# Moving the convolution's weight products from VectorE to GpSimd in a gated attention and state-space kernel

## The chip, the cores and the metric

The kernel runs on one core of a Trainium2 chip. A core has five engines that this document calls TensorE (PE in the profile, its weight loads PEld), VectorE (DVE), ScalarE (ACT), GpSimd (POOL) and SyncE (SP, which here only issues DMAs). Each works through its own list of instructions in order and waits on semaphores for the others. The metric is the device time of one execution in microseconds (us), as the median of several runs.

## The reference

Two branches share one input x of 2048 rows by 512 columns (bf16), and a gate per row mixes them. Branch A is full softmax attention with 32 heads of 16 columns. Branch B is a long convolution: each of 512 channels has a kernel K that is the sum over 128 complex modes of C times dB times the l-th power of exp(dt A), for 2048 values of l. In the reference it is done by FFT.

```python
g = _sigmoid((x * gate_w).sum(-1, keepdims=True))
a = _A_ref(x, A_wqkv, A_wo)          # softmax(q k^T / 4) v per head, then @ wo
b = _B_ref(x, ...)                   # y = causal convolution of x with K, plus x * Dskip
return g * a + (1 - g) * b
# in _B_ref:
dt = jnp.exp(log_dt)[:, None]
P = jnp.exp(logdA[:, :, None] * l[None, None, :])
K = jnp.einsum("dn,dnl,dn->dl", Cc, P, dB).real
```

## The kernel before

**Attention.** The scores are cut into 2048 tiles of 128 keys by 512 queries: 32 blocks of a query chunk and a group of heads, 16 key tiles in a block, four head strips in each. Three tiles make a group (683 of them, numbered g): TensorE writes the group's scores into one of two score buffers in PSUM, SC, ScalarE takes the exponential into a ring of 14 slots, ET (EX with it late in the program), and TensorE multiplies by the values into the one output bank OA. When a block is done, VectorE transposes OA into OT, which empties the bank for the next block. ScalarE runs one exponential per group and so takes the groups' order along.

**Quads.** Part of the exponentials are done by VectorE instead. In a *quad*, four consecutive groups leave their third tile to VectorE. It writes an approximation into the bits of an integer (`bits`, L982: tile DZ from SC) and, after four, makes three shifted copies of all four (`batch`, L996: DU from DZ, 2048 columns). TensorE adds DZ and the DUs up with four matmuls a tile (`sums`). `decide` and `win` say at which groups a quad starts: WIN lists the stretches of groups, how many DZ buffers there are and the least distance of two starts; SL is the distance while the convolution's blocks are behind, which KX and KB define; RX and RATE cap how many quads there may be by group x; and a budget of VectorE's idle time must be there.

**Convolution.** From A, dt, B and C the program makes powers L1 to L80 and M1 to M9 of exp(dt A) (`params`, `params2`), and the products WW = C dt B and WN = WW M1, where M1 is the conjugated 128th power. For each quarter qr of the 512 channels, `powers` makes the table B16 and `weights` the first 8 rows of Z, starting from copies of WW and WN in the scratch FP and going by M2 and M4 with the scratch tiles ft1 and ft2. Quarters 1 to 3 are made early, in `bases`, in staging tiles (B16s, Zbs) that are stored to DRAM (`store`, L1320); quarter 0 is made in `tables`, which then completes each Z (`zpart`), multiplies B16 into the tables T, and starts `kstage`, where TensorE forms K for 32 channels at a time. K goes to DRAM; `yloads` brings it back as H with the rows of x as U; `ystage` convolves. `xrows` puts x into DRAM in the order that U needs: GpSimd clears the margin of tile xP, SP transposes x into it 16 times (L1430), and 16 stores follow (L1435).

**The order of the work.** The program is written in Python that keeps its own clock for each engine. Background work is a set of threads, each with a priority (a lower number goes first); a thread's step names its engine and planned cost, and may wait for a mark (AFTER) or hold a lock (LOCK: `powers`, `weights` and `zpart` share "FT", because they share FP, ft1 and ft2). Between groups, `fill` issues the steps that fit. What results is one fixed list per engine, with waits on semaphores where data cross engines. GpSimd's list holds only memsets and two iotas. SBUF is laid out afterwards from the lifetimes of the tiles, in groups.

Of the kernel before, what the change touches and what calls it, by code (L numbers as in the profile page):

```python
# [6 lines left out]
FP32 = mybir.dt.float32  # L7
# [8 lines left out]
D = 512  # L16
# [33 lines left out]
XS = 128 * DH ** -.5 / math.log(2)  # L50
CUTS = (26, 56, 94)
XB = 128 * (127 - math.log2(5.3794))
WIN = ((110,560,2,5,0,1),(560,674,4,5,0,2))
EARLY = 3
YLP = 4.5
RATE = 5.3
KA = -2
KX = 100
SL = 9
YQ = 0  # L60
KB = 26
RX = 100
RATE2 = 5.3
XR = 560
XGO = 'g14'
YGO = 'projs'
YLGO = 'K15'
TGO = 'bw31'
BPR = 2
KP = .2  # L70
NB = 1
# [64 lines left out]
class Prog:  # L136
# [113 lines left out]
    def op(self, eng, fn, R=(), W=(), c=.1, lat=.085, a=0, cfg=None):  # L250
        if self.cap is not None:
            self.cap.append((self.op, (eng, fn, R, W), dict(c=c, lat=lat, a=a, cfg=cfg)))
            return
        if cfg is not None:
            if cfg != self.cfg:
                c += TURN[cfg]
            self.cfg = cfg
        self.act += a
        self.log.append((self.op, self.q, (eng, fn, R, W)))
        deps = self._deps(eng, R, W)  # L260
        i = self.cnt[eng]
        at = self.tm[eng]
        for s, k in deps.items():
            at = max(at, self.fin[(s, k)] + (.03 if s == eng else .05))
        if eng == "PE" and len(self.pt) + 1 >= self.edge():
            at = max(at, self.land())
        self.tm[eng] = at + c
        if eng == "DVE":
            self.busy += c
        self.fin[(eng, i)] = at + c + lat  # L270
        self.cnt[eng] += 1
        w = self._record(eng, fn, deps, eng, i, R, W)
        if eng == "PE":
            b = self.edge()
            self.pt += [at] * (2 + max(w - 1, 0))
            if len(self.pt) > b:
                self.av.append(max(self.pt[b - LEAD] + F1, self.av[-1] + F2))
        return at + c + lat
# [219 lines left out]
def declare(nc, es):  # L498
    B = {}

    def sb(name, free, dt=BF16):
        B[name] = Buf(name, "sb", free, dt)
# [56 lines left out]
        sb("D" + n, 2 * D)  # L559

    sb("FP", 2 * 128 * 8, FP32)
    sb("ft1", 2 * 64 * 8, FP32)
    sb("ft2", 2 * 64 * 8, FP32)
    for k in range(NB):
# [112 lines left out]

def dap(t, off, dims):
    return bass.AP(tensor=t, offset=off, ap=[list(d) for d in dims])


def dv(n, r=1):
# [3 lines left out]
def record(nc, p, B, ins):  # L686
# [352 lines left out]
    def tt(eng, o, a, b_, f, R, W, c):  # L1039
        op(eng, lambda v: v.tensor_tensor(o(), a(), b_(), f), R, W, c=c)  # L1040
# [4 lines left out]
    def key(*ns):  # L1045
        return [(B[n], 0) for n in ns]
# [63 lines left out]

    def params2():
        yield ("AFTER", "L2")
        seq = [("u1", "BreT", "dt", ALU.mult), ("u2", "BimT", "dt", ALU.mult), ("u3", "CreT", "u1", ALU.mult),
               ("u4", "CimT", "u2", ALU.mult), (0, "u3", "u4", ALU.subtract), ("u3", "CreT", "u2", ALU.mult),
               ("u4", "CimT", "u1", ALU.mult), (1, "u3", "u4", None)]
        for o, a, b_, f in seq:
            yield ("DVE", F5)
            if f is None:
                op("DVE", lambda v: v.scalar_tensor_tensor(B["WW"](D, [[1, D]]), B["u3"](0, [[1, D]]), -1.0, B["u4"](0, [[1, D]]),
                                                           ALU.mult, ALU.subtract), key("u3", "u4"), key("WW"), c=F5)  # L1120
            elif o == 0:
                tt("DVE", half(B["WW"], 0), full(a), full(b_), f, key(a, b_), key("WW"), F5)
            else:
                tt("DVE", full(o), full(a), full(b_), f, key(a, b_), key(o), F5)
        yield ("AFTER", "L32")
        yield from short("L32", "c")
        yield from short("L16", "n")
        yield ("AFTER", "M1")
        yield from cmul("WN", "WW", "M1")
        sch.mark("WN")  # L1130
        yield from short("L64", "n")
        yield from cmul("L80", "L64", "L16")
        yield ("AFTER", "M8")
        yield from cmul("M9", "M8", "L32", "xc")
        yield from short("M8", "")
        yield from short("M9", "")
        yield from short("L80", "n")

    FT = [B["ft1"], B["ft2"]]
    HF = [(0,), (1,), (0, 1)]  # L1140
# [6 lines left out]

    def weights(qr, last, top):

        FP = B["FP"]  # L1150
        d0, e8, l8 = 128 * qr, 128 * 8, last.free // 2
        rw = lambda *k: [(FP, x) for x in k]

        def cast(part, l):
            yield ("DVE", .3)
            op("DVE", lambda v: v.tensor_copy(last(part * l8 + 128 * l, [[1, 256]]), FP(part * e8 + 128 * l, [[1, 256]])), rw(l, l + 1), top, c=.21)

        def mul(i, m, ln):
            ts = 128 * m
            yield ("DVE", dv(2 * ts))  # L1160
            tt("DVE", lambda: ft(i, 2, 0, [[ts, 2], [128, m], [1, 128]]), lambda: FP(0, [[e8, 2], [128, m], [1, 128]]),
               lambda: B[ln](i * D + d0, [[0, 2], [0, m], [1, 128]]), ALU.mult, rw(*range(m)) + key(ln), ftk(i, 2), dv(2 * ts))

        def add(part, m, out, W):
            ts = 128 * m
            yield ("DVE", dv(ts))
            tt("DVE", out, lambda: ft(0, 2, part * ts, [[1, ts]]), lambda: ft(1, 2, (1 - part) * ts, [[1, ts]]),
               ALU.add if part else ALU.subtract, ftk(0, 2) + ftk(1, 2), W, dv(ts))

        yield ("LOCK", "FT")  # L1170
        for l, n in enumerate(("WW", "WN")):
            yield ("DVE", .25)
            op("DVE", lambda v, l=l, n=n: v.tensor_copy(FP(128 * l, [[e8, 2], [1, 128]]), B[n](d0, [[D, 2], [1, 128]])), key(n), rw(l), c=.25)
        yield from mul(0, 2, "M2")
        yield from mul(1, 2, "M2")
        yield from cast(0, 0)
        yield from add(0, 2, lambda: FP(256, [[1, 256]]), rw(2, 3))
        yield from add(1, 2, lambda: FP(e8 + 256, [[1, 256]]), rw(2, 3))
        yield from cast(1, 0)
        yield from mul(0, 4, "M4")  # L1180
        yield from mul(1, 4, "M4")
        yield from cast(0, 2)
        yield from add(0, 4, lambda: last(512, [[1, 512]]), top)
        yield from add(1, 4, lambda: last(l8 + 512, [[1, 512]]), top)
        yield from cast(1, 2)
        sch.unlock("FT")

    def powers(qr, last, top, *tag):

# [110 lines left out]

    bd = B["bd"]

    def bases():
        yield ("AFTER", "L8")
        for qr in range(1, 4):
            for k, (t, W) in enumerate(((B["B16s"], 2048), (B["Zbs"], 1024))):
                keys = [(t, x, (qr, k)) for x in ((0, 2, (1, 0), (1, 4)) if k == 0 else (0,))]
                if qr > 1:
                    yield ("AFTER", f"bw{qr - 1}{k}")
                if k == 0:  # L1310
                    yield from powers(qr, t, keys[:2], (qr, 0))
                else:
                    if qr == 1:
                        yield ("AFTER", "WN")
                        yield ("AFTER", "M4")
                    yield from weights(qr, t, keys)
                later("SP", .6, 2, lambda t=t, k=k, W=W, qr=qr, keys=keys: store(t, k, W, qr, keys))

    def store(t, k, W, qr, keys):
        dma("SP", lambda e: e.dma_start(bd.dram((2 * qr + k) * P * 4096, [[4096, P], [W, 2], [1, W]]), t(0, [[W, 2], [1, W]])),  # L1320
# [6 lines left out]
    def tables():  # L1327
        H5 = dv(512, 2)
        yield ("AFTER", TGO)
        for qr in range(4):  # L1330
            B16, Z = B[f"B16{qr % NB}"], B[f"Z{qr % NZ}"]
            if qr == 0:
                yield from powers(qr, B16, [(B16, 0), (B16, 2)])
                yield from weights(qr, Z, [(Z, 3, qr), (Z, 5, qr)])
            else:
                yield ("AFTER", f"bw{qr}1")
                for k, ky in enumerate((0, 2, (1, 0), (1, 4))):
                    yield ("SP", .6)
                    dma("SP", lambda e, B16=B16, qr=qr, k=k: e.dma_start(B16(1024 * k, [[1, 1024]]), bd.dram(2 * qr * P * 4096 + 1024 * k, [[4096, P], [1, 1024]])),
                        [(bd, (qr, 0))], [(B16, ky)], c=.6, lat=3, b=.95, pace=True)  # L1340
                if qr >= NZ:
                    yield ("AFTER", f"KT{4 * (qr - NZ) + 3}")
                for k in range(2):
                    yield ("SP", .6)
                    dma("SP", lambda e, Z=Z, qr=qr, k=k: e.dma_start(Z(4096 * k, [[1, 1024]]), bd.dram((2 * qr + 1) * P * 4096 + 1024 * k, [[4096, P], [1, 1024]])),
                        [(bd, (qr, 1))], [(Z, 3 + 2 * k, qr)], c=.6, lat=3, b=.95, pace=True)
# [377 lines left out]
    sch.mark("Q0.0")  # L1724
    sch.mark("qm0")

    for th, pr in ((norms(), 0), (qms(), 0), (projs(), .3), (gate(), .25), (ystage(), 2), (yloads(), 4), (params(), 2), (params2(), 2),
                   (tables(), 2), (bases(), BPR), (xrows(), 4), (outs(), 6)):
        sch.add(th, pr)

    def need(g):
# [125 lines left out]
```

## Time and profile before

| | |
|---|---|
| median of 3 runs | 793.34 us (792.64 to 793.35) |
| profiled execution, own time | 796.0 us |
| its span | 794.2 us |
| granted TensorE clock | 0.992 |
| busy: ScalarE, VectorE, TensorE, GpSimd | 776.1, 740.0, 694.1, 11.3 us |

The span runs from the first to the last instruction of the profiled execution, and its own time has 1.8 us around it. A row of a group of instructions names the line, engine and operation, the tile written and the tiles read, the shape, how many there are, then busy time, the mean duration of one in ns, and the engine's idle time in front of them with what ended it. Neighbours on one engine overlap, so busy time divided by the count is less than the mean duration. A row that begins with two numbers and a colon between them is a stretch of the span: its length, then the busy time and count of each engine, the granted clock, the share of DMA and its GB/s; asked for one engine and one tile, only those instructions are counted. Rows that give three durations with slashes list least, median and largest duration in ns and the first and last start in us.

### The profile page before, as it was taken

How to read it: one execution, taken by the hardware profiler on the slowest of the kernel's cores; microseconds unless marked ns; L12 is line 12 of the kernel's file. 1: busy time of each engine (PE TensorE's matmuls, PEld its weight loads, DVE VectorE, ACT ScalarE, POOL GpSimd, SP SyncE). 2: the span in 40 equal slices, each digit the busy share in tenths (PEclk: the TensorE clock that was granted, in tenths of full speed). 3: DMA queues.
4: the chain of work that ended last, by engine and by line, in shares of the span. 5: the costliest groups of instructions: out<-in, count | busy, mean ns of one | idle time of the engine just before them, and what ended most of it. 6: DMA issues, size and time to landing. Idle time of an engine off the chain costs nothing.

```text
span 794.2 us, 31538 instructions
## 1 busy us (share of the span) xinstructions
PE 694.1 (87%) x14177; PEld 293.9 (37%) x14178; DVE 740.0 (93%) x1291; ACT 776.1 (98%) x694; POOL 11.3 (1%) x21
## 2 busy tenths in 40 slices
PE   8777787798878889899899899999899999989996
PEld 3223332222224434455344454444454444422222
DVE  7999999999999799989999999999989979899993
ACT  7999999999999999999999999999999999999995
POOL 5000000000000000000000000000000000000000
PEclk9999999999999999999999999999899999999999
DMA  9454211211011666764636764677847568720001
GB/s 211 84 107 76 63 55 72 110 38 43 5 58 27 181 159 176 199 154 118 187 93 171 204 162 121 175 176 184 210 127 184 142 153 218 193 64 31 25 21 34
DMA packets 138281, 95.52 MB, mean 120 GB/s; under 512 B 86049, under 2 KB 117154, under 8 KB 137762
## 3 DMA queue, kind: packets, MB, share of 16 engines
q1 hardware_dynamic: 136130, 92.32, 45.4%
q8 instruction: 111, 1.82, 1.0%
q10 hardware_dynamic: 2016, 1.18, 0.7%
q14 instruction: 24, 0.20, 0.1%
HBM read 65.38 MB, written 19.42 MB: 107 GB/s over the span
## 4 chain that ended last, share of the span: by engine, by line
ACT 88%; PE 5%; DVE 3%; DMA 3%; SPq 1%; issue 0%; DVEq 0%
ACT ET L961 80%; ACT EX L961 7%; DMA H<-gm_kd 2%; PE SC L701 2%; PE OA L701 2%; PE MB L701 1%; DVE DZ L982 1%; SPq L1453 1%; DVE DU L996 1%; DMA gm_kd<-Ks 1%; DVE T L1040 0%; SPq L1465 0%; DVE Yst L1497 0%; DVE Kt L1402 0%; DVE Ks L1406 0%
## 5 line engine op out<-in xcount | busy, mean ns | idle before, releaser
L961 ACT ACTIVATE ET<-SC 128x1536 bf16<-128x1536 f32 (+1 forms) x615 | 702.5, 1473 | 4.0 <-PE SC L701 3.7
L701 PE MATMUL SC<-Qm,KT 32*128 32x512 bf16 x2048 | 274.7, 386 | 83.3 <-ACT ET L961 71.4
L982 DVE TENSOR_SCALAR DZ<-SC 128x512 uint16<-128x512 f32 x356 | 237.7, 683 | 22.1 <-PE SC L701 20.6
L996 DVE TENSOR_SCALAR DU<-DZ 128x2048 uint16<-128x2048 uint16 x267 | 174.2, 685 | 0.5
L701 PEld LDWEIGHTS SC<-Qm,KT 32*128 32x128 bf16 x2048 | 70.1, 91 | 282.5 <-ACT ET L961 223.9
L701 PE MATMUL OA<-wm 128*32 128x256 bf16 (+3 forms) x903 | 159.7, 342 | 1.2 <-DVE wm L754 1.2
L701 PE MATMUL OA<-ET,VE 128*32 128x512 bf16 x1533 | 158.2, 389 | 0.9 <-ACT ET L961 0.9
L701 PE MATMUL OA<-DU,VE 128*32 128x512 bf16 x1068 | 101.1, 388 | 0.0
L701 PEld LDWEIGHTS MB<-U,H 128*32 128x32 bf16 x4096 | 82.7, 144 | 26.8 <-issue 15.6
L701 PE MATMUL MB<-U,H 128*32 128x128 bf16 (+7 forms) x4096 | 88.5, 226 | 2.4 <-DMA H<-gm_kd 2.4
L961 ACT ACTIVATE EX<-SC 128x1024 bf16<-128x1024 f32 (+1 forms) x68 | 80.0, 1376 | 1.1 <-PE SC L701 1.1
L701 PEld LDWEIGHTS OA<-ET,VE 128*32 128x32 bf16 x1533 | 40.5, 94 | 74.8 <-issue 70.6
L1040 DVE TENSOR_TENSOR T<-B,DT 128x1536 bf16<-128x1536 bf16 x64 | 58.4, 948 | 0.0
L701 PEld LDWEIGHTS MB<-T,Z 128*32 128x32 bf16 x2048 | 45.3, 154 | 11.6 <-issue 6.3
L701 PEld LDWEIGHTS OA<-wm 128*32 128x32 bf16 (+2 forms) x903 | 42.3, 95 | 16.3 <-issue 13.5
L701 PE MATMUL MB<-T,Z 128*32 128x64 bf16 (+1 forms) x2048 | 47.4, 235 | 0.0
L701 PEld LDWEIGHTS OA<-DU,VE 128*32 128x32 bf16 x1068 | 27.2, 97 | 32.6 <-issue 21.1
L701 PE MATMUL OA<-DZ,VE 128*32 128x512 bf16 x356 | 35.6, 389 | 0.0
L1016 DVE STREAM_TRANSPOSE OT<-OA 128x512 f32<-128x512 f32 x32 | 22.7, 708 | 9.1 <-PE OA L701 9.1
L1497 DVE TENSOR_TENSOR Yst<-MB,gt 128x512 bf16<-128x512 f32 x32 | 22.0, 686 | 6.3 <-PE MB L701 6.1
L701 PE MATMUL OA<-EX,VE 128*32 128x512 bf16 x159 | 23.0, 399 | 0.3 <-ACT EX L961 0.3
L1040 DVE TENSOR_TENSOR ft<-Z,DM 128x1024 bf16<-128x1024 bf16 x32 | 21.3, 677 | 0.0
(145 smaller groups left out, 447.7 us busy)
## 6 DMA issues: line engine op xcount, KB each, us to landing
H<-gm_kd SPq DMA_DIRECT2D x128, 256.0 KB, 4.1
U<-gm_xs SPq DMA_DIRECT2D x128, 134.2 KB, 3.4
T<-B SPq DMA_DIRECT2D x16, 256.0 KB, 3.4
gm_yd<-Yst SPq DMA_DIRECT2D x64, 64.0 KB, 2.9
gm_bd<-B16s SPq DMA_DIRECT2D x3, 1024.0 KB, 4.5
B<-gm_bd SPq DMA_DIRECT2D x12, 256.0 KB, 3.9
gm_kd<-Ks SPq DMA_DIRECT2D x64, 40.0 KB, 3.1
gm_xs<-xP SPq DMA_DIRECT2D x16, 136.0 KB, 4.0
```

What stands on the lines that cost most here:

```text
L701: op("PE", lambda t: t.matmul(out(), lhsT(), rhs(), start=start, stop=stop, skip_group_check=True, **kw), R, W, c=c, lat=.15, a=a, cfg=cfg)
L961: op("ACT", lambda a: a.activation(E(at, [[1, 512 * n]]), sc(0, [[1, 512 * n]]), AF.Exp, scale=DH ** -0.5), [(sc, i, g) for i in range(n)] ...
L982: op("DVE", lambda v: v.tensor_scalar(z.u16(512 * k, [[1, 512]]), sc(1024, [[1, 512]]), XS, XB, ALU.mult, ALU.add), [(sc, 2, g)], [(z, k, ...
L996: op("DVE", lambda v, u=u, cut=cut: v.tensor_scalar(u.u16(0, [[1, 2048]]), z.u16(0, [[1, 2048]]), float(cut), None, ALU.add), R, [(u, 0, i ...
L1016: op("DVE", lambda v: v.transpose(OT(512 * w, [[1, 512]]), OA(0, [[1, 512]])), [(OA, 0, b)], [(OT, w, b)], c=.64)
L1040: op(eng, lambda v: v.tensor_tensor(o(), a(), b_(), f), R, W, c=c)
L1453: dma("SP", lambda e, v=v, U=U, i=i: e.dma_start(U(UP * i, [[1, UN]]), xs.dram((v // 2 * 32 + v % 2 * 4) * UW + 2 * UP * i + R8 - 1, [[D * ...
L1497: op("DVE", lambda v, w=w, h=h: v.tensor_tensor(Yst(1024 * w + 4 * h, [[128, R8], [8, 16], [1, 4]]), MB(0, [[1, R8], [R8, 16], [NC, 4]]), ...
```

## The change

`weights` moves from VectorE to GpSimd, in buffers of its own: FW in place of FP, fw1 and fw2 in place of ft1 and ft2, half the length, so that it no longer takes the lock. A new thread, `wchain`, makes WW and WN on GpSimd; the same steps leave `params2`. `bases` is split into two threads, one for powers (VectorE) and one for weights (GpSimd); the latter also makes the weights of quarter 0 in Z0, at the end, and `tables` waits for that. The planned cost of a GpSimd instruction of n elements is `pl(n)`. The conjugation at the end of WW was one instruction (multiply and subtract) and becomes an addition and a multiplication by -1. Constants change: quads may start from group 80 instead of 110 and until 678 instead of 674, with the pacing constants KX, SL and RX changed; the x rows start after group 70 instead of group 14; `tables` starts after the third store of powers (bw30) instead of the third store of weights (bw31). The plan has 97 quads.

```diff
-WIN = ((110,560,2,5,0,1),(560,674,4,5,0,2))
+WIN = ((80,560,2,5,0,1),(560,678,4,5,0,2))
-KX = 100
-SL = 9
+KX = 90
+SL = 11
-RX = 100
+RX = 60
-XGO = 'g14'
+XGO = 'g70'
-TGO = 'bw31'
+TGO = 'bw30'
...
+    sb("FW", 2 * 128 * 4, FP32)
+    sb("fw1", 2 * 128 * 4, FP32)
+    sb("fw2", 2 * 128 * 4, FP32)
...
+def pl(n):
+    return .12 + n / 420
...
-        yield ("AFTER", "M1")
-        yield from cmul("WN", "WW", "M1")
-        sch.mark("WN")
...
+    def wchain():
+        H = pl(512)
+        t1, t2 = B["u3"], B["u4"]
+        for o, a, b_, f in (("u1", "BreT", "dt", ALU.mult), ("u2", "BimT", "dt", ALU.mult), ("u3", "CreT", "u1", ALU.mult),
+                            ("u4", "CimT", "u2", ALU.mult), (0, "u3", "u4", ALU.subtract), ("u3", "CreT", "u2", ALU.mult),
+                            ("u4", "CimT", "u1", ALU.mult), ("u3", "u3", "u4", ALU.add)):
+            yield ("POOL", H)
+            tt("POOL", half(B["WW"], 0) if o == 0 else full(o), full(a), full(b_), f, key(a, b_), key("WW" if o == 0 else o), H)
+        yield ("POOL", H)
+        op("POOL", lambda v: v.tensor_scalar(B["WW"](D, [[1, D]]), t1(0, [[1, D]]), -1.0, None, ALU.mult), key("u3"), key("WW"), c=H)
+        yield ("AFTER", "M1")
...
+        sch.mark("WN")
...
     def weights(qr, last, top):
-        FP = B["FP"]
-        d0, e8, l8 = 128 * qr, 128 * 8, last.free // 2
+        FP, FW = B["FW"], [B["fw1"], B["fw2"]]
+        d0, e4, l8 = 128 * qr, 128 * 4, last.free // 2
...
         def mul(i, m, ln):
             ts = 128 * m
-            yield ("DVE", dv(2 * ts))
-            tt("DVE", lambda: ft(i, 2, 0, [[ts, 2], [128, m], [1, 128]]), lambda: FP(0, [[e8, 2], [128, m], [1, 128]]),
-               lambda: B[ln](i * D + d0, [[0, 2], [0, m], [1, 128]]), ALU.mult, rw(*range(m)) + key(ln), ftk(i, 2), dv(2 * ts))
+            yield ("POOL", pl(2 * ts))
+            tt("POOL", lambda: FW[i](0, [[ts, 2], [128, m], [1, 128]]), lambda: FP(0, [[e4, 2], [128, m], [1, 128]]),
+               lambda: B[ln](i * D + d0, [[0, 2], [0, m], [1, 128]]), ALU.mult, rw(*range(m)) + key(ln), [(FW[i], 0)], pl(2 * ts))
...
-        yield ("LOCK", "FT")
...
-    def bases():
-        yield ("AFTER", "L8")
+    def bases(k, t, W):
+        yield ("AFTER", "WN" if k else "L8")
+        if k:
+            yield ("AFTER", "M4")
...
+        if k:
+            Z = B["Z0"]
+            yield from weights(0, Z, [(Z, 3, 0), (Z, 5, 0)])
+            sch.mark("W0")
...
             if qr == 0:
                 yield from powers(qr, B16, [(B16, 0), (B16, 2)])
-                yield from weights(qr, Z, [(Z, 3, qr), (Z, 5, qr)])
+                yield ("AFTER", "W0")
...
-    for th, pr in ((norms(), 0), (qms(), 0), (projs(), .3), (gate(), .25), (ystage(), 2), (yloads(), 4), (params(), 2), (params2(), 2),
-                   (tables(), 2), (bases(), BPR), (xrows(), 4), (outs(), 6)):
+    for th, pr in ((norms(), 0), (qms(), 0), (projs(), .3), (gate(), .25), (ystage(), 2), (yloads(), 4), (params(), 2), (params2(), 2), (wchain(), 1.5),
+                   (tables(), 2), (bases(0, B["B16s"], 2048), BPR), (bases(1, B["Zbs"], 1024), 1.5), (xrows(), 4), (outs(), 6)):
```

More of the change, by code (lines that the diff above doesn't have):

```diff
@@ L1112, in params2 @@
         yield ("AFTER", "L2")
[L1113 to L1124, printed above, removed]
         yield ("AFTER", "L32")
@@ L1137, in params2 @@
         yield from short("L80", "n")
+    def wchain():
[9 more added lines that the diff above has]
+        yield ("AFTER", "M1")
+        x, y = B["WW"], B["M1"]
+        w1, w2 = B["fw1"], B["fw2"]
+        for t, ri in ((w1, 0), (w2, 1)):
+            yield ("POOL", pl(1024))
+            tt("POOL", lambda t=t: t(0, [[1, 2 * D]]), lambda: x(0, [[1, 2 * D]]), lambda ri=ri: y(ri * D, [[0, 2], [1, D]]), ALU.mult,
+               [(x, 0), (y, 0)], [(t, 0)], pl(1024))
+        for k, f in ((0, ALU.subtract), (1, ALU.add)):
+            yield ("POOL", H)
+            tt("POOL", half(B["WN"], k), half(w1, k), half(w2, 1 - k), f, [(w1, 0), (w2, 0)], key("WN"), H)
+        sch.mark("WN")
     FT = [B["ft1"], B["ft2"]]
@@ L1148, in weights @@
     def weights(qr, last, top):
-        FP = B["FP"]
-        d0, e8, l8 = 128 * qr, 128 * 8, last.free // 2
+        FP, FW = B["FW"], [B["fw1"], B["fw2"]]
+        d0, e4, l8 = 128 * qr, 128 * 4, last.free // 2
         rw = lambda *k: [(FP, x) for x in k]
         def cast(part, l):
-            yield ("DVE", .3)
-            op("DVE", lambda v: v.tensor_copy(last(part * l8 + 128 * l, [[1, 256]]), FP(part * e8 + 128 * l, [[1, 256]])), rw(l, l + 1), top, c=.21)
+            yield ("POOL", .7)
+            op("POOL", lambda v: v.tensor_copy(last(part * l8 + 128 * l, [[1, 256]]), FP(part * e4 + 128 * l, [[1, 256]])), rw(l, l + 1), top, c=pl(256))
@@ L1164, in add @@
         def add(part, m, out, W):
             ts = 128 * m
-            yield ("DVE", dv(ts))
-            tt("DVE", out, lambda: ft(0, 2, part * ts, [[1, ts]]), lambda: ft(1, 2, (1 - part) * ts, [[1, ts]]),
-               ALU.add if part else ALU.subtract, ftk(0, 2) + ftk(1, 2), W, dv(ts))
-        yield ("LOCK", "FT")
+            yield ("POOL", pl(ts))
+            tt("POOL", out, lambda: FW[0](part * ts, [[1, ts]]), lambda: FW[1]((1 - part) * ts, [[1, ts]]),
+               ALU.add if part else ALU.subtract, [(FW[0], 0), (FW[1], 0)], W, pl(ts))
@@ L1171, in weights @@
         for l, n in enumerate(("WW", "WN")):
-            yield ("DVE", .25)
-            op("DVE", lambda v, l=l, n=n: v.tensor_copy(FP(128 * l, [[e8, 2], [1, 128]]), B[n](d0, [[D, 2], [1, 128]])), key(n), rw(l), c=.25)
+            yield ("POOL", .7)
+            op("POOL", lambda v, l=l, n=n: v.tensor_copy(FP(128 * l, [[e4, 2], [1, 128]]), B[n](d0, [[D, 2], [1, 128]])), key(n), rw(l), c=pl(256))
         yield from mul(0, 2, "M2")
         yield from mul(1, 2, "M2")
+        yield from add(0, 2, lambda: FP(256, [[1, 256]]), rw(2, 3))
@@ L1176, in weights @@
+        yield from add(1, 2, lambda: FP(e4 + 256, [[1, 256]]), rw(2, 3))
         yield from cast(0, 0)
-        yield from add(0, 2, lambda: FP(256, [[1, 256]]), rw(2, 3))
-        yield from add(1, 2, lambda: FP(e8 + 256, [[1, 256]]), rw(2, 3))
         yield from cast(1, 0)
@@ L1181, in weights @@
         yield from mul(1, 4, "M4")
-        yield from cast(0, 2)
         yield from add(0, 4, lambda: last(512, [[1, 512]]), top)
         yield from add(1, 4, lambda: last(l8 + 512, [[1, 512]]), top)
+        yield from cast(0, 2)
         yield from cast(1, 2)
-        sch.unlock("FT")
     def powers(qr, last, top, *tag):
@@ L1301, in record @@
     bd = B["bd"]
-    def bases():
-        yield ("AFTER", "L8")
+    def bases(k, t, W):
+        yield ("AFTER", "WN" if k else "L8")
+        if k:
+            yield ("AFTER", "M4")
         for qr in range(1, 4):
[L1306 to L1317, printed above, removed]
+            keys = [(t, x, (qr, k)) for x in ((0,) if k else (0, 2, (1, 0), (1, 4)))]
+            if qr > 1:
+                yield ("AFTER", f"bw{qr - 1}{k}")
+            if k:
+                yield from weights(qr, t, keys)
+            else:
+                yield from powers(qr, t, keys[:2], (qr, 0))
+            later("SP", .6, 2, lambda qr=qr, keys=keys: store(t, k, W, qr, keys))
+        if k:
+            Z = B["Z0"]
+            yield from weights(0, Z, [(Z, 3, 0), (Z, 5, 0)])
+            sch.mark("W0")
     def store(t, k, W, qr, keys):
```

## The prediction

> **What bounds the kernel now.** I read the busy shares first, then the slices of the span, the chain, the groups by shape, and last the stretch in which the change works.
>
> ```profile
> span 794.2 us, 31538 instructions
> PE 694.1 (87%) x14177; PEld 293.9 (37%) x14178; DVE 740.0 (93%) x1291; ACT 776.1 (98%) x694; POOL 11.3 (1%) x21
> POOL 5000000000000000000000000000000000000000
> ACT 88%; PE 5%; DVE 3%; DMA 3%; SPq 1%; issue 0%; DVEq 0%
> ```
>
> ScalarE (ACT) is busy for 776.1 of 794.2 us and is 88% of the chain: the exponentials set the time. VectorE has 54 us left in the whole span, GpSimd is empty after the first slice. Where VectorE's 54 us lie matters more than their sum:
>
> ```profile
> core 0: us, PE busy (x) PEld busy (x) DVE busy (x) ACT busy (x) POOL busy (x), PEclk, DMA share, GB/s
> 26.00:160.00 134.00, 105.30 (x2064) 38.67 (x2064) 129.10 (x245) 134.00 (x102) 0.00 (x0) 1.00 0.32 82
> 160.00:260.00 100.00, 84.03 (x1264) 26.99 (x1260) 97.37 (x171) 99.97 (x90) 0.00 (x0) 1.00 0.11 33
> 740.00:794.00 54.00, 45.30 (x549) 12.73 (x550) 40.67 (x70) 46.19 (x44) 0.00 (x0) 0.98 0.08 26
> ```
>
> From 26 to 160 us, where the weights are made, ACT never stops and VectorE has 4.9 us free in 134. Both are full there, and every instruction of VectorE stands in one written order, so a VectorE that falls behind takes ACT with it: it is VectorE that empties the output bank at each block's end and that frees the third score tile of a quad's group.
>
> **The change, part by part.** *Quads.* A quad sends four tiles from ACT to VectorE; its four groups shrink from three tiles to two on ACT. The rows count 356 tiles, that is 89 quads.
>
> ```profile
> L961 ACT ACTIVATE ET<-SC 128x1536 bf16<-128x1536 f32 x303 | 433.7, 1724 | 2.9 <-PE SC L701 2.8
> L961 ACT ACTIVATE ET<-SC 128x1024 bf16<-128x1024 f32 x312 | 315.4, 1229 | 1.1 <-PE SC L701 0.8
> L982 DVE TENSOR_SCALAR DZ<-SC 128x512 uint16<-128x512 f32 x356 | 237.7, 683 | 22.1 <-PE SC L701 20.6
> L996 DVE TENSOR_SCALAR DU<-DZ 128x2048 uint16<-128x2048 uint16 x267 | 174.2, 685 | 0.5
> L701 PE MATMUL OA<-DU,VE 128*32 128x512 bf16 x1068 | 101.1, 388 | 0.0
> ```
>
> By busy time, which leaves the overlap of neighbours out, a three-tile instruction costs 433.7/303 = 1.431 us and a two-tile one 315.4/312 = 1.011. The title's 97 quads are eight more: 32 groups x 0.420 = 13.4 us off ACT. VectorE gets 32 x 237.7/356 = 21.4 plus 24 x 174.2/267 = 15.7, together 37.1 us. TensorE gets twelve more matmuls a quad, 96 x 101.1/1068 = 9.1 us; it has 100 us free and runs filler matmuls which give way, so I cost that at nothing. Should that cover go, its price is those 9.1 us.
>
> *Work taken from VectorE.* Everything that makes WW, WN and the four sets of weights leaves:
>
> ```profile
> L1040 DVE TENSOR_TENSOR ft<-FP,M 128x1024 f32<-128x1024 f32 x8 | 9.7, 1217 | 0.0
> L1040 DVE TENSOR_TENSOR ft<-FP,M 128x512 f32<-128x512 f32 x8 | 5.2, 689 | 0.1
> L1040 DVE TENSOR_TENSOR FP<-ft,ft 128x256 f32<-128x256 f32 x16 | 6.7, 420 | 0.2
> L1040 DVE TENSOR_TENSOR Zbs<-ft,ft 128x512 bf16<-128x512 f32 x6 | 4.1, 685 | 0.2
> L1156 DVE CAST Zbs<-FP 128x256 bf16<-128x256 f32 x12 | 3.4, 286 | 0.0
> L1040 DVE TENSOR_TENSOR Z<-ft,ft 128x512 bf16<-128x512 f32 x2 | 1.4, 692 | 0.1
> L1156 DVE CAST Z<-FP 128x256 bf16<-128x256 f32 x4 | 1.1, 288 | 0.0
> L1173 DVE COPY FP<-WN 128x256 f32<-128x256 f32 x4 | 1.1, 286 | 0.0
> L1040 DVE TENSOR_TENSOR pt<-WW,M 128x1024 f32<-128x1024 f32 x2 | 2.4, 1218 | 0.0
> L1040 DVE TENSOR_TENSOR WN<-pt,pt 128x512 f32<-128x512 f32 x2 | 1.4, 686 | 0.0
> L1040 DVE TENSOR_TENSOR u<-CimT,u 128x512 f32<-128x512 bf16 x2 | 1.4, 685 | 0.0
> ```
>
> Half of the third row is the powers' own and stays. The copies from WW are as many as those from WN (1.1). Weights: 9.7 + 5.2 + 3.35 + 4.1 + 3.4 + 1.4 + 1.1 + 2.2 = 30.45 us in 56 instructions. WW and WN: 2.4 + 1.4, and eight of 512 elements, of which the last row shows two, at 0.7 = 5.6; so 9.4 us in 12 instructions. Together 39.9 us go and 37.1 come: VectorE's own work falls by 2.8 us, to 737. As sums, all of it fits.
>
> *The same work on GpSimd.* 13 instructions make WW and WN (the last step of WW becomes two), 14 make each set of weights: 69, over 7680 + 4 x 6144 = 32256 elements in a partition's row. No row shows GpSimd reading anything. The nearest are its memsets:
>
> ```profile
> 2.28 7.68 POOL L771 MEMSET VE<- 128x2240 bf16 x4 [0.32 <-DVE piota L759]
> L771 POOL MEMSET VE<- 128x2240 bf16 x4 | 7.7, 1965 | 0.3 <-DVE piota L759 0.3
> L1427 POOL MEMSET xP<- 128x256 bf16 x4 | 1.1, 312 | 0.0
> 7.84 0.68 DVE L1040 TENSOR_TENSOR bn<-AimT,dt 128x512 f32<-128x512 bf16 x1
> ```
>
> They give (1965 - 312) / (2240 - 256) = 0.833 ns an element and 99 ns an instruction: 33.7 us in all, a lower bound, as these instructions also read. The upper bound is the diff's own planning figure, 0.12 us and 420 elements a microsecond: 85.1 us. I take the middle, 59.4, because two operands are read where the memset reads none. In the Trainium skill, GPSIMD Engine Reference, section Elementwise — side-by-side cycle accounting, an addition of 2048 fp32 elements takes 4497 ns; an estimate from it is 71 us, and by it the sum below would be 823; no run here shows it.
>
> *Where that time lies.* The rows are the first reader of Z0, GpSimd's last product; the last operand's load with its time to landing; the chain's first stretch of ACT; and the x rows with what uses them.
>
> ```profile
> L1040 DVE TENSOR_TENSOR ft<-Z,DL x16: 671/682/693, 220.2 to 544.6; 128x1024 bf16<-128x1024 bf16 x16
> L720 SPq DMA_TRANSPOSE CimT<-in_B_C_im_dram x1: 1261/1261/1261, 22.7 to 22.7; - x1
> DMA to landing us min/median/max: 3.5/3.5/3.5
> 13.47 68.50 ACT ET L961 x51
> L1430 SPq DMA_TRANSPOSE xP<-in_A_x_dram x16: 1189/1267/2402, 25.1 to 49.9; - x16
> L1435 SPq DMA_DIRECT2D gm_xs<-xP x16: 359/372/1124, 51.5 to 67.6; - x16
> L1453 SPq DMA_DIRECT2D U<-gm_xs x128: 514/597/2047, 186.8 to 683.3; - x128
> L1497 DVE TENSOR_TENSOR Yst<-MB,gt x32: 674/684/693, 273.6 to 696.2; 128x512 bf16<-128x512 f32 x32
> ```
>
> The last operand lands at 22.7 + 3.5 = 26 us, so GpSimd works from 26 to at latest 26 + 85 = 111 us, some 120 with the waits for Zbs' three stores. All of it is beside the VectorE that has 4.9 us free. Taken alone it is hidden: Z0 is not read before 220 us.
>
> *What the two engines do to each other.* Price per GpSimd instruction for VectorE: nothing at the one end, the whole GpSimd instruction at the other, whenever VectorE's next instruction also reads SBUF. At the lower end stands the addition at 7.84 us, which ran beside a memset in its usual 0.68. That memset writes and does not read; every moved instruction reads. What VectorE could go on with is what reads PSUM:
>
> ```profile
> 26.00:160.00 134.00, 25.41 (x37) 1.00 0.32 82
> 26.00:160.00 134.00, 3.56 (x5) 1.00 0.32 82
> 26.00:160.00 134.00, 0.69 (x1) 1.00 0.32 82
> ```
>
> These are VectorE's instructions on MB, on OA and on DZ: 29.7 of its 129.1 us. The other 77% read SBUF, nearly all additions and products that already draw two operands at a time. Between the two ends I take the upper, since the single row at the lower one lacks the very thing that would collide. It is a judgement. Cost: 0.77 x 59.4 = 45.7 us of VectorE waiting. Of that VectorE's own gaps swallow 4.9, and ACT's lead, 14 ring slots at three a group, 14/3 x 1.431 = 6.7. What is left, 34.1 us, ACT stands still, and gets it back nowhere, as it is the bound from there on. The rule for it is in the Trainium skill, SBUF — State Buffer, section Who interferes with whom: a VectorE instruction with two SBUF inputs contends with a GpSimd instruction that reads SBUF, not with one that only writes, and the later one blocks until the other has ended; by it the sum is 814, without it 780; the trace agrees as far as its write-only memsets go, and cannot show the rest.
>
> *Other edits, at nothing.* The x rows move from group 14 to group 70, some 13.5 + 71 x 68.50/51 = 109 us. They took 25 to 68 us on SP's queue, so they end near 152, ahead of the first U load at 186.8; the four memsets of xP now queue behind GpSimd's weights, and SP's row stores and the query loads behind them wait if those are late, which has some 35 us of cover, the same as U. Zbs' stores now wait for GpSimd; behind them on SP stand query loads that are issued a block, 28 us, ahead. The gate's memset is needed with the first Yst, past 270 us. Powers no longer wait for the weights' lock, which is what lets quads start at group 80.
>
> **Sum.** Own time 796.0 (span 794.2) - 13.4 = 782.6; the runs' median stands 2.7 below the profiled execution, so 779.9 without collision. With it 779.9 + 34.1 = 814.0. By the bounds of GpSimd's time: 0.77 x 33.7 - 11.6 = 14.3, so 794; 0.77 x 85.1 - 11.6 = 53.9, so 834. VectorE's own account agrees: 737 + 46 busy or waiting and about 30 us idle at both ends and late is 813.
>
> **The rivals.** *The engines pass each other by* (faster). Same counts, no waiting: 780. For it speaks the row at 7.84 us; against it that it is one row without reads. It decides at 13.4 + 11.6 = 25.0 us of lost VectorE time, 0.36 us for each of the 69: below that the kernel is faster.
>
> *GpSimd is the one that waits.* If VectorE always goes first, GpSimd's end moves from 120 us by 0.53 us (129.1/245) for each VectorE instruction let past. Z0 is read at 220 less the 39.9 us taken out, 180. The 60 us between are used up at 1.7 instructions let past each; at 2.2, GpSimd ends at 200 and VectorE, with ACT behind it, waits 20 us: 800. Against it: it needs all 69 held up twice.
>
> *The change does less than it says.* A quad that is not made costs 4 x 0.42 = 1.7 us; without collision all eight would have to be missing for no gain. Nothing in the rows speaks for it, VectorE's sum fits, and I give it no chance of its own.
>
> **How the numbers follow.** Collision with VectorE waiting: 0.55, 814, own range 794 to 834. Passing by: 0.37, 780. GpSimd late: 0.08, 800. Two executions differ here by about 0.1%, so 0.2% (1.6 us) is what can be told from no change. Slower: 0.53 of the first case and 0.05 of the third, 0.58; same: 0.02 and 0.01; faster: 0.37 and 0.02. The range must take in both signs: 778, just under 780, to 836, just over the upper bound of GpSimd's time.
>
> **What would show it.** Right: 388 DZ rows and 291 DU rows; two-tile ACT rows up by 32; GpSimd busy from 26 us on; VectorE's SBUF additions longer than 683 ns or gaps in front of them while GpSimd works, its PSUM casts not; ACT idle between 40 and 160 us. Wrong: the additions stay at 683 ns and ACT at 134.00 of 134, then 780; or a gap in front of the first product on Z, then 800. GpSimd instructions far dearer than 420 elements a microsecond would take the time past my range.

## The result and the profile after

The changed kernel takes 827.07 us (826.79 to 828.65, four runs); the kernel beside it took 793.14 (792.64 to 793.35). The ratio is 1.0433, 95% interval 1.0415 to 1.0451: 34 us slower, where 814 was forecast. The profiled execution took 826.79 with a span of 825.0.

From the page of the changed kernel: the span, the busy shares, two rows of the 40 slices, the shares of the chain.

```profile
span 825.0 us, 31588 instructions
PE 706.3 (86%) x14156; PEld 297.1 (36%) x14156; DVE 785.7 (95%) x1279; ACT 765.1 (93%) x694; POOL 109.0 (13%) x90
ACT  7776586989999999999999999999999999999995
POOL 4789928200000000000000000000000000000000
ACT 70%; DVE 23%; PE 5%; DMA 1%; issue 1%; ACTq 0%; DVEq 0%
```

ScalarE's work fell by 11.0 us, where eight more quads were forecast to save 13.4, but its idle time went from 18.1 us (794.2 - 776.1) to 59.9 (825.0 - 765.1). The slices say where: ACT's gaps lie where POOL works, and ACT is at 9 from then on. VectorE's busy time *rose* by 45.7 us, though by the sum of its instructions it should have fallen by 2.8; and 23% of the chain now runs over VectorE. The stretches, with the columns of the prediction's table:

```profile
26.00:160.00 134.00, 86.26 (x1575) 32.21 (x1572) 132.53 (x164) 95.24 (x71) 95.37 (x72) 0.83 0.13 40
160.00:260.00 100.00, 89.46 (x1123) 24.62 (x1119) 95.82 (x169) 94.89 (x89) 0.00 (x0) 0.97 0.30 74
```

VectorE is busy for 132.5 of 134 us and gets through 164 instructions, where it got through 245. ScalarE works 95 of the 134 us, and the 39 that it idles are most of the 42 that it idles more in all. VectorE's instructions have become longer; from the groups by shape, first before, then after:

```profile
L1087 DVE CAST DT<-L 128x2048 bf16<-128x2048 f32 x3 | 3.7, 1220 | 0.0
L1201 DVE COPY FP<-L 128x256 f32<-128x256 f32 x12 | 3.4, 286 | 0.0
L1040 DVE TENSOR_TENSOR M<-pt 128x512 f32<-128x512 f32 x4 | 2.7, 674 | 0.0
L807 DVE CAST VE<-MB 128x512 bf16<-128x512 f32 x16 | 11.1, 691 | 1.7 <-PE MB L701 0.9 <-PE SC L701 0.6
```

```profile
L1094 DVE CAST DT<-L 128x2048 bf16<-128x2048 f32 x3 | 6.9, 2286 | 0.0
L1213 DVE COPY FP<-L 128x256 f32<-128x256 f32 x12 | 7.5, 622 | 0.1
L1047 DVE TENSOR_TENSOR M<-pt 128x512 f32<-128x512 f32 x4 | 5.1, 1263 | 0.0
L814 DVE CAST VE<-MB 128x512 bf16<-128x512 f32 x16 | 10.9, 680 | 0.3 <-PE MB L708 0.3
```

The three rows that read SBUF have about doubled; the cast from PSUM is as it was. For every VectorE shape that both kernels have, I take the busy time after, less the busy time before at the same count. These differences add up to 47.8 us: that is VectorE's waiting. It lies inside the instructions' durations, not in gaps in front of them. One place in the two timelines shows how it comes about:

```profile
66.54 6.06 DVE L1047 TENSOR_TENSOR pt<-L,L 128x1024 f32<-128x1024 f32 x2
65.44 6.08 POOL L1047 TENSOR_TENSOR fw<-FW,M 128x1024 f32<-128x1024 f32 x2
```

Two VectorE products of 1024 columns, 1.22 us each before, last 6.06 us together, interleaved with two GpSimd products of the same length. How it reached ScalarE is in the list of waits (waiter, line, what ended the wait, us in total, times, longest):

```profile
ACT ET L968 <- PE SC L708: 43.6, 28, 6.7
PEld MB L708 <- DVE VE L814: 22.8, 9, 6.9
PE MB L708 <- DVE VE L814: 20.5, 9, 6.6
POOL Zbs L1170 <- DMA gm_bd<-Zbs: 15.6, 1, 15.6
PEld OA L708 <- DVE OT L1023: 11.6, 7, 5.4
POOL fw L1047 <- DVE M L1047: 7.2, 1, 7.2
PEld MB L708 <- DVE KT L805: 8.5, 6, 3.6
```

ScalarE waits for scores; TensorE, which makes them, stands in front of a projection, because the one bank MB still waits for VectorE's cast of the last projection (VE, KT), up to 6.9 us at a time. The scores stand behind that projection in TensorE's list. The PEld and PE rows are largely the same stalls, seen at the weight load and at the matmul, and are not to be added. The transpose of OA is the smaller part.

The stall is not the whole of it. Here are the same 48 matmuls of a projection at two places, the second behind a long stall, with what follows there; then a later stretch in the columns of the table above:

```profile
38.29 0.85 PE L708 MATMUL MB<-Wv,xT 128*32 128x128 bf16 x48 [1.07 <-DVE KT L805]
92.89 1.47 PE L708 MATMUL MB<-Wv,xT 128*32 128x128 bf16 x48 [6.50 <-DVE VE L814]
94.30 0.61 PE L708 MATMUL SC<-Qm,KT 32*128 32x512 bf16 x3
94.98 4.34 ACT L968 ACTIVATE ET<-SC 128x1536 bf16<-128x1536 f32 x3 [6.69 <-PE SC L708]
166.50:173.30 6.80, 6.77 (x50) 1.19 (x50) 4.79 (x9) 4.07 (x6) 0.00 (x0) 0.50 0.41 79
```

TensorE goes on at 92.89 us, but ScalarE only at 94.98, because the projection that was held up and the scores come first. Both run slowly: the granted TensorE clock is 0.50 from 88.0 to 98.2 us, a stretch that begins while TensorE stands still (from 86.4 us). There are eight such stretches from 29.9 to 173.3 us, 51 us in all, and they hold 26 of the 44 us that ScalarE idles between 26 and 260 us. In the last, shown above, GpSimd has ended long before (at 150 us) and TensorE is busy throughout, and yet ScalarE works only 4.1 of 6.8 us. So a TensorE that was starved comes back at half the clock and for a while can't keep ScalarE at work. How much of the loss is the clock's own, no run here separates.

### The profile page after: what moved, and what is told of

The parts are those of the page before. It is cut to its first block, busy times and chain, and to the rows that moved or that the text cites. A ratio compares the mean times of both kernels' runs of the same rounds, so it can differ in the third digit from the quotient of the medians.

```text
span 825.0 us, 31588 instructions
## 1 busy us (share of the span) xinstructions
PE 706.3 (86%) x14156; PEld 297.1 (36%) x14156; DVE 785.7 (95%) x1279; ACT 765.1 (93%) x694; POOL 109.0 (13%) x90
## 4 chain that ended last, share of the span: by engine, by line
ACT 70%; DVE 23%; PE 5%; DMA 1%; issue 1%; ACTq 0%; DVEq 0%
ACT ET L968 62%; ACT EX L968 8%; DVE pt L1047 3%; DVE DZ L989 3%; DVE ft L1047 2%; PE SC L708 2%; DVE DU L1003 1%; PE OA L708 1%; DVE FP L1047 1%; DVE KT L805 1%; DVE VE L814 1%; PE MB L708 1%; DVE L L1047 1%; DVE B16s L1244 1%; DMA Wk<-in_A_wqkv_dram 1%; DVE DT L1094 1%
## 5 line engine op out<-in xcount | busy, mean ns | idle before, releaser
L968 ACT ACTIVATE ET<-SC 128x1024 bf16<-128x1024 f32 (+1 forms) x616 | 695.9, 1384 | 46.7 <-PE SC L708 43.6
L708 PE MATMUL SC<-Qm,KT 32*128 32x512 bf16 x2048 | 279.2, 391 | 61.1 <-ACT ET L968 50.2
L989 DVE TENSOR_SCALAR DZ<-SC 128x512 uint16<-128x512 f32 x388 | 259.9, 682 | 16.3 <-PE SC L708 14.2
L1003 DVE TENSOR_SCALAR DU<-DZ 128x2048 uint16<-128x2048 uint16 x291 | 190.1, 683 | 0.7
L708 PE MATMUL OA<-wm 128*32 128x256 bf16 (+3 forms) x781 | 152.5, 353 | 1.2 <-DVE wm L761 1.2
L708 PE MATMUL OA<-DU,VE 128*32 128x512 bf16 x1164 | 110.5, 386 | 0.2
L708 PE MATMUL MB<-T,Z 128*32 128x48 bf16 (+1 forms) x2048 | 47.7, 235 | 0.0
L708 PE MATMUL MB<-Wv,xT 128*32 128x128 bf16 x1024 | 23.7, 244 | 27.0 <-DVE VE L814 20.1
L1047 POOL TENSOR_TENSOR fw<-FW,M 128x512 f32<-128x512 f32 (+1 forms) x16 | 36.2, 2279 | 0.4
L708 PEld LDWEIGHTS MB<-Wv,xT 128*32 128x32 bf16 x1024 | 18.8, 108 | 34.4 <-DVE VE L814 22.8
```

The costliest lines, as they stand in the source:

```text
L708: op("PE", lambda t: t.matmul(out(), lhsT(), rhs(), start=start, stop=stop, skip_group_check=True, **kw), R, W, c=c, lat=.15, a=a, cfg=cfg)
L968: op("ACT", lambda a: a.activation(E(at, [[1, 512 * n]]), sc(0, [[1, 512 * n]]), AF.Exp, scale=DH ** -0.5), [(sc, i, g) for i in range(n)] ...
L989: op("DVE", lambda v: v.tensor_scalar(z.u16(512 * k, [[1, 512]]), sc(1024, [[1, 512]]), XS, XB, ALU.mult, ALU.add), [(sc, 2, g)], [(z, k, ...
L1003: op("DVE", lambda v, u=u, cut=cut: v.tensor_scalar(u.u16(0, [[1, 2048]]), z.u16(0, [[1, 2048]]), float(cut), None, ALU.add), R, [(u, 0, i ...
```

## The experiments

**The moved instructions write, and read nothing.** Each of them in the changed kernel becomes two memsets of its output; plan, quads, orders and waits are the changed kernel's.

```diff
     def tt(eng, o, a, b_, f, R, W, c):
-        op(eng, lambda v: v.tensor_tensor(o(), a(), b_(), f), R, W, c=c)
+        if eng == "POOL":
+            op("POOL", lambda v: v.memset(o(), 0.0), R, W, c=c / 2, lat=0.0)
+            op("POOL", lambda v: v.memset(o(), 0.0), R, W, c=c / 2 - .03)
+        else:
+            op(eng, lambda v: v.tensor_tensor(o(), a(), b_(), f), R, W, c=c)
```

> The changed kernel with every moved GpSimd instruction replaced by two memsets of its output: the plan, the quads, the order of every engine and all waits stay, but GpSimd reads nothing (so the weights, and with them the convolution's kernel K, are left out: zeros). Collision of reads: VectorE's products of 512 columns are back at about 683 ns, ScalarE idles under 3 us between 26 and 160 us, and the time is 780 us (776 to 786). Rival, the plan itself is slow (early quads, late x rows, VectorE's or TensorE's new order): 815 to 830, with the durations of VectorE back to normal and ScalarE idle as before. Rival, any GpSimd instruction holds VectorE up, reading or not: memsets take about 0.9 times as long as the work they replace, so VectorE is held for some 30 us and the time is about 805.

Measured: 786.23 us beside 793.47, ratio 0.9911 (0.9878 to 0.9944). Busy shares, the stretch, and three of VectorE's rows:

```profile
PE 691.8 (88%) x14156; PEld 294.0 (38%) x14156; DVE 742.9 (95%) x1279; ACT 763.2 (97%) x694; POOL 85.3 (11%) x159
26.00:160.00 134.00, 109.28 (x2069) 38.93 (x2061) 130.84 (x237) 131.71 (x109) 71.69 (x137) 0.99 0.30 77
L1101 DVE CAST DT<-L 128x2048 bf16<-128x2048 f32 x3 | 3.8, 1275 | 0.0
L1054 DVE TENSOR_TENSOR M<-pt 128x512 f32<-128x512 f32 x4 | 2.7, 673 | 0.0
L1251 DVE CAST B16s<-FP 128x512 bf16<-128x512 f32 x12 | 8.1, 675 | 0.1
```

With GpSimd busy for 71.7 us of the same stretch, but not reading, the products are at 673 ns, ScalarE idles 2.3 us there, and the kernel is 0.9% faster than before. The reading costs 827.07 - 786.23 = 41 us. That this run computes with zeros does not explain them: 40 of them are ScalarE's work within the first 260 us (250.8 us here, 210.7 in the changed kernel), and the first product on Z comes at 205 us here and at 247 there. The plan is not what is slow, and the granted TensorE clock, which had sunk to 0.83 in this stretch, is 0.99 again: it had fallen with the starved TensorE. Part of the third theory holds as well: the casts B16s<-FP stay long, 675 ns against 450 before, and VectorE's rows are still 4.6 us longer than before in all. The time lies 6 us above the 780 expected, just past the range. Of these, 2.4 are idle time of ScalarE (783.7 - 763.2 = 20.5 us, 18.1 before) and 0.5 its smaller saving; the other 3.4 come from the step by which the forecast went from the profiled execution to the median (2.7 us; here the profiled execution lay 0.7 below the median).

**GpSimd work added to the kernel before.** 69 instructions of the moved kinds and sizes, on columns of KT, into a tile that nobody reads; then only the first 35.

```diff
+    def extra():
+        yield ("AFTER", "L2")
+        yield ("AFTER", "K0.2")
...
+        for f, n in seq[:69]:
+            yield ("POOL", .12 + n / 420)
+            if f == "t":
+                op("POOL", lambda v, n=n: v.tensor_tensor(z(0, [[1, n]]), KT(0, [[1, n]]), KT(512, [[1, n]]), ALU.mult), R, key("dz"), c=.12 + n / 420)
+            else:
+                op("POOL", lambda v, n=n: v.tensor_copy(z(0, [[1, n]]), KT(0, [[1, n]])), R, key("dz"), c=.12 + n / 420)
```

> The kernel before with 69 GpSimd instructions of the moved kinds and sizes (products, sums and copies of bf16 columns of KT into a scratch tile that nothing reads) added from about 24 us on; the other engines' lists are untouched. Collision of reads: VectorE waits about 45 us, of which ScalarE feels 34 to 42, so 793 + 34 to 42 = 827 to 835; the VectorE rows that read SBUF are longer, the casts from PSUM are not. Rival, the changed plan is what costs: 793, no row longer than before.

> As the run with 69 added instructions, but only the first 35 of them, 16384 of 32256 elements. Collision of reads: about half of VectorE's waiting, 23 us; the fixed cover (ScalarE's lead, VectorE's gaps) is nearly used up once, so ScalarE loses 12 to 20 and the time is 805 to 813. Were it a fixed cost of waking GpSimd up, it would cost as much as all 69.

Measured: 839.08 us with 69, ratio 1.0574 (1.0534 to 1.0614); 816.48 with 35, ratio 1.0292 (1.0255 to 1.0329). VectorE's waiting, summed up as above, is 42.4 and 21.4 us. The stretch of the first:

```profile
26.00:160.00 134.00, 89.02 (x1529) 31.72 (x1517) 130.46 (x156) 92.05 (x69) 88.85 (x73) 0.76 0.22 51
PEld MB L702 <- DVE KT L799: 29.0, 10, 7.2
```

Work that nobody needs makes the kernel before 46 us slower and gives the picture of the changed kernel: fewer and longer VectorE instructions, TensorE in front of a projection. Half of it costs half. The cost also came out above both expectations, 839 and 816 against at most 835 and 813: I had allowed for more cover than there is. ScalarE's idle time rose by 41.5 us ((837.8 - 778.2) - 18.1) for 42.4 us of VectorE's waiting, so almost none was covered.

**Pairs of instructions alone.** A kernel that only runs eight VectorE instructions of one kind beside GpSimd instructions of one kind, stage by stage. It was measured once.

```python
STAGES = [(d, q, 512) for d in DVE for q in ("none", "two")]
STAGES += [(d, q, 512) for d in ("two", "cast", "quad") for q in ("copy", "fill")]
STAGES += [("two", "two", n) for n in (128, 256, 1024, 2048)]
```

> No part of the reference is computed: in 24 stages VectorE runs eight instructions of one kind while GpSimd runs none, or instructions of one kind, beside them. VectorE: two = product of two fp32 SBUF operands, 512 columns; twoh = the same in bf16, 1024; cast = fp32 to bf16 within SBUF; quad = 16-bit addition of a constant, 2048; psum = cast from PSUM; mix = product of a PSUM and an SBUF operand; turn = transpose of bf16. GpSimd: product of two operands, copy, fill (memset), 512 elements, and the product also with 128, 256, 1024 and 2048. Collision of reads by whole instructions: two, twoh, cast and quad beside a GpSimd product last 1.0 to 1.8 us in the mean in place of 0.68, and the wait grows in proportion to the GpSimd instruction's length (by some 0.3 us at 128 elements, 2 to 5 us at 2048); psum, mix and turn stay as alone; fill leaves two as alone. Rival, the two share by bandwidth and not by whole instructions: two is longer by the same factor at 128 and at 2048 elements. Rival, fill also holds cast and quad up: then their write side collides too.

From the timeline (start, length of the row's instructions together, output's name = VectorE's kind and GpSimd's):

```profile
7.67 5.78 DVE L54 TENSOR_TENSOR o_two_none<-a,b 128x512 f32<-128x512 f32 x8
13.47 12.36 DVE L54 TENSOR_TENSOR o_two_two<-a,b 128x512 f32<-128x512 f32 x8
13.59 16.04 POOL L69 TENSOR_TENSOR z<-x,y 128x512 f32<-128x512 f32 x10 [7.33 <-DVE o_two_none L54]
51.81 3.66 DVE L58 CAST o_cast_none<-a 128x512 bf16<-128x512 f32 x8 [3.90 <-POOL z L69]
97.94 5.77 DVE L62 CAST o_psum_two<-ps 128x512 bf16<-128x512 f32 x8
98.05 13.32 POOL L69 TENSOR_TENSOR z<-x,y 128x512 f32<-128x512 f32 x10 [6.01 <-DVE o_psum_none L62]
117.27 5.77 DVE L64 TENSOR_TENSOR o_mix_two<-ps,a 128x512 f32<-128x512 f32 x8
136.80 5.94 DVE L65 STREAM_TRANSPOSE o_turn_two<-ah 128x512 bf16<-128x512 bf16 x8
150.33 8.21 DVE L54 TENSOR_TENSOR o_two_copy<-a,b 128x512 f32<-128x512 f32 x8 [7.59 <-POOL z L69]
159.80 5.78 DVE L54 TENSOR_TENSOR o_two_fill<-a,b 128x512 f32<-128x512 f32 x8 [1.25 <-POOL z L71]
173.20 5.95 DVE L58 CAST o_cast_fill<-a 128x512 bf16<-128x512 f32 x8 [1.92 <-POOL z L71]
```

In the stages with GpSimd products of 512, VectorE's first instruction has started before GpSimd's first (13.47 us against 13.59) and takes its usual time; only the other seven wait. So the price is read from single instructions, by their least, median and largest duration in ns. The rows are a product, a cast and the 16-bit addition beside GpSimd products of 512 columns, then a product beside GpSimd products of 128, 256, 1024 and 2048:

```profile
L54 DVE TENSOR_TENSOR o_two_two<-a,b x8: 693/1632/1632, 13.5 to 24.2; 128x512 f32<-128x512 f32 x8
L58 DVE CAST o_cast_two<-a x8: 427/1368/1369, 55.5 to 64.4; 128x512 bf16<-128x512 f32 x8
L60 DVE TENSOR_SCALAR o_quad_two<-ah x8: 695/1632/1634, 75.9 to 86.6; 128x2048 uint16<-128x2048 uint16 x8
L54 DVE TENSOR_TENSOR o_two_two<-a,b x8: 825/826/976, 199.0 to 205.2; 128x512 f32<-128x512 f32 x8
L54 DVE TENSOR_TENSOR o_two_two<-a,b x8: 1093/1096/1245, 222.9 to 230.9; 128x512 f32<-128x512 f32 x8
L54 DVE TENSOR_TENSOR o_two_two<-a,b x8: 692/2710/2859, 241.5 to 256.8; 128x512 f32<-128x512 f32 x8
L54 DVE TENSOR_TENSOR o_two_two<-a,b x8: 692/693/4866, 257.6 to 271.0; 128x512 f32<-128x512 f32 x8
```

Beside a GpSimd product of 512, a VectorE product takes 1.63 us in place of 0.69, a cast 1.37 in place of 0.43, the 16-bit addition 1.63 in place of 0.69. The surcharge is 0.94 us each time, whatever VectorE's instruction is. Instructions with an operand in PSUM, and the transpose, take none (eight took 5.77 and 5.93 us alone). A GpSimd copy of 512 charges a product 0.29; a memset charges a product nothing, but a cast 0.28 and the 16-bit addition as much, which is what was left in the first experiment. With GpSimd products of 128, 256, 1024 and 2048 (the last four rows) a product's surcharge is 0.13, 0.40, 2.02 and 4.17 us: it goes with the length of GpSimd's instruction, not with VectorE's, at 2.1 ns an element. So it is a wait for whole instructions and no sharing of bandwidth, by which the product would be longer by the same factor at 128 and at 2048. But it is less than the GpSimd instruction, which takes 1.33 us beside the PSUM cast (13.32 / 10). GpSimd waits too: its ten products take 16.04 us beside VectorE's products. This bears out the rule in the Trainium skill, SBUF — State Buffer, section Who interferes with whom, as to which pairs collide, the memset beside the two kinds included; that the later instruction waits for all of the earlier one is more than was measured here, 0.94 of 1.33 us and 4.17 of 4.88.

**The same amount late.** 32256 elements again, in instructions of at most 512, but behind the exponential of group 300.

```diff
+        yield ("AFTER", "g300")
...
+                op("POOL", lambda v, n=n: v.tensor_tensor(z(0, [[1, n]]), KT(0, [[1, n]]), KT(512, [[1, n]]), ALU.mult), [(KT, (0, 0)), (KT, (0, 1)), (B["tk"], 300)], key("dz"), c=.12 + n / 420)
```

> The kernel before with GpSimd instructions of the same 32256 elements (47 products of 512, 8 of 256, 24 copies of 256) added from the exponential of group 300 on, at about 352 us, in the stretch of quads; the other engines' lists are untouched. There 46.4 of VectorE's 96.1 us in 352 to 452 us (DZ, MB, OA) read PSUM. If every GpSimd instruction ends up holding VectorE, whatever it does first, since it lasts longer than any PSUM instruction: by the pairs measured alone 47 x 0.82 + 8 x 0.42 + 24 x 0.15 = 46 us of waiting at most, some 42 as in the early run, and 793 + 35 to 42 = 828 to 835. If it is VectorE's share of SBUF time that decides, as the prediction had it: 0.52 x 46 = 24 us, 793 + 18 to 24 = 811 to 817.

Measured: 821.18 us, ratio 1.034 (1.0314 to 1.0365); VectorE's waiting is 27.1 us. Of its rows:

```profile
L983 DVE TENSOR_SCALAR DZ<-SC 128x512 uint16<-128x512 f32 x356 | 237.7, 683 | 20.7 <-PE SC L702 19.1
L997 DVE TENSOR_SCALAR DU<-DZ 128x2048 uint16<-128x2048 uint16 x267 | 193.7, 757 | 0.5
```

DZ, which reads PSUM, is untouched at 237.7 us; DU, which reads SBUF, took 19.5 us longer (174.2 before). 27 us is near the 24 of the theory that goes by VectorE's share of SBUF time and far from 42, so the share does decide. The 0.82 us of the expectation is an average over eight instructions, the first of which had not waited. With the surcharges of the single instructions (and 0.15 us for a copy of 256, an estimate from the 0.29 of a copy of 512) the pairs add up to 52.4 us for the 69 instructions, 27.2 for the 35 and 51.0 for the late ones. The measured waiting is 42.4 / 52.4 = 0.81, 21.4 / 27.2 = 0.79 and 27.1 / 51.0 = 0.53 of it, where VectorE's share of SBUF time is 0.77, 0.77 and 0.52. The time lies above the range of that theory by 4 us, all the same: it rose by 27.4 us, so here too nothing was covered. A product of 512 in this stretch costs VectorE 0.53 x 0.94 = 0.50 us, in place of about 0.60 from one start to the next if VectorE does it itself; early it costs 0.81 x 0.94 = 0.76. That is an estimate, and no run tried such a move.

**The constants alone.** Before, with the changed windows and pacing; the x rows stay at group 14, and `tables` starts as before.

```diff
-WIN = ((110,560,2,5,0,1),(560,674,4,5,0,2))
+WIN = ((80,560,2,5,0,1),(560,678,4,5,0,2))
-KX = 100
-SL = 9
+KX = 90
+SL = 11
-RX = 100
+RX = 60
```

> The kernel before with the changed constants alone (WIN from 80 and to 678, KX 90, SL 11, RX 60), without the GpSimd part and with the x rows still at group 14, as the layout in SBUF does not hold with them at group 70. The plan then has 88 quads in place of 89. If quads come from VectorE time that the weights leave free: 792 to 797, no gain. Rival, earlier quads and the new pacing are a gain or a loss by themselves: outside 790 to 799.

Measured: 798.38 us (795.67 to 799.82), ratio 1.0055 (1.0032 to 1.0078). There are 88 quads (352 DZ rows), so the added quads do come from VectorE's freed time: earlier windows alone bring none. A loss of 4.6 us is more than the 1.7 us of the missing quad. It lies above the first theory's range (to 797) and does not reach the other's (over 799), so neither was met; its cause stays open.

## Why the prediction was right

The direction and the mechanism were right: VectorE waits for GpSimd's reads, and ScalarE pays. The time came out 13 us above 814; the largest part of that, 5.6 us, is cover that was not there. By its steps:

- *Quads.* 388 DZ and 291 DU, 32 more two-tile instructions, as said. ScalarE's saving of 13.4 us is 12.9 where nothing collides (776.1 - 763.2 in the write-only run) and 11.0 in the changed kernel, where a three-tile instruction costs 399.0/275 = 1.451 us of busy time in place of 1.431, presumably because next to a gap there is no neighbour to overlap with.
- *Work taken from VectorE.* Right: 737 was forecast without collision; the write-only run shows 742.9, of which 4.6 are its longer rows.
- *GpSimd's own time, 59.4 us.* Too small. By the pairs, 1.33 us for 512 and about 2.3 ns per further element (4.88 for 2048), the 69 instructions come to some 76 us alone (an estimate from these rows), nearer to the diff's 85 and to the estimate of 71 by the Trainium skill's GPSIMD Engine Reference, Elementwise — side-by-side cycle accounting, than to my middle of the memset's price and the diff's. In the changed kernel they took 97.7 (109.0 - 11.3), since GpSimd waits for VectorE too, as it did in the pairs.
- *VectorE's waiting, 0.77 x 59.4 = 45.7 us.* Measured 47.8, but the product came right by luck, with two errors against each other: the time was 76, and a GpSimd product of 512 holds VectorE only for 0.94 of its 1.33 us. By the pairs the whole is 52.4, and 0.77 of that is 40; 42.4 were measured with the added instructions and 47.8 in the changed kernel, and what makes up the last 5 is open. The judgement that the colliding end of the bounds holds because the memset beside the addition lacks the reads is borne out by the write-only run and the pair two/fill.
- *Cover, 11.6 us.* This is the term that was wrong. ScalarE's idle time rose by 41.8 us for the 47.8 of waiting, so 6 were covered, and in the run with 69 added instructions only 1. I had counted ScalarE's lead in the ring; but ScalarE does not run out of ring (2.2 us of waits for TensorE's work on OA), it runs out of scores (43.6 us), because TensorE stands in its list in front of a projection whose bank VectorE has not emptied, and comes back at half the clock. I had named the output bank and the quads' tiles as the path and not this one. The path is read from the waits; no run took it away.
- The rest of the 13 us: 5.6 from the cover, 2.1 from the waiting, 2.4 from ScalarE's smaller saving, and 3.0 because I carried over that the profiled execution of before lay 2.7 above its median; that of after lay 0.3 below its own.
- *GpSimd late* did not happen: it ended at about 150 us, and Z0 is first read at 247. *Other edits, at nothing*: nearly held, in that the write-only run has them all and ScalarE idles only 2.4 us more in it than before; the constants alone cost 4.6. One estimate was off: GpSimd waited 15.6 us for a store of Zbs, the margin of xP stood behind it in GpSimd's list, and the x rows were stored by 196 us and not by 152. The first U load came at 251, so they were in time.

## What to carry to other kernels

Work moved from a full VectorE to GpSimd is not free even where GpSimd is idle: a GpSimd instruction that reads SBUF holds VectorE up wherever VectorE's next instruction draws two operands from SBUF or runs a fast copy, cast or 16-bit constant within it; so compare the surcharge (0.94 us for a product of 512), weighted by the share of VectorE's time that reads SBUF, with the time that VectorE saves (0.6 us). By these figures, an estimate, a move of this kind can pay only where less than 0.6 / 0.94 = 0.64 of VectorE's time reads SBUF, or with writes alone. And a lead in a ring buffer is no cover when an in-order engine between the two stands in front of something else that the late engine must free.

## What was not expected of the hardware

- The surcharge does not depend on VectorE's instruction (0.94 us for a product, a cast and a 16-bit addition) and is less than GpSimd's instruction: 0.13, 0.40, 0.94, 2.02 and 4.17 us for 128 to 2048 elements.
- The waiting is shown inside the VectorE instruction's duration, with hardly a gap in front. A VectorE that looks busier with the same work is waiting.
- The granted TensorE clock in 26 to 160 us fell with TensorE's work: 0.83 in the changed kernel and 0.76 with 69 added instructions, against 1.00 before and 0.99 with writes alone. It fell in stretches at 0.50, in which a busy TensorE no longer keeps ScalarE at work (4.1 of 6.8 us).
